# One PSUM bank a tile in the expert stage: first layers in two banks each, dense and expert halves of second layers in banks of their own

## The chip, the cores and the metric

The kernel is written in Bass with the Tile framework and runs on one core of a Trainium2 chip. The metric is the device time of one execution in microseconds (us). Before the change the median of three runs is 907.2 us (905.64 to 908.45).

The core's engines each work off their own queue of instructions in order: TensorE (PE) for matmuls, with its weight loads shown apart (PEld); VectorE (DVE); ScalarE (ACT); GpSimd (POOL); SyncE (SP), which here only starts transfers. They wait for each other through semaphores. TensorE writes its results into PSUM, which in this kernel is cut into eight banks of 128 partitions x 512 f32.

## The reference

Two stages, one after the other, over 8 batches of 2816 rows (22528 rows in all), with 256 channels and 64 query-key channels:

```python
# attention, for each batch
scores = (1 / S) * z @ z.T              # z: (2816, 64)
attn   = np.maximum(scores, 0.0) ** 2
x      = u * (attn @ v)                 # u, v: (2816, 256)

# mixture of experts over all rows x: (22528, 256)
y_dense    = np.maximum(x @ w1_dense, 0.0) @ w2_dense        # 256 -> 512 -> 256
logits     = x @ w_gate                                      # 8 experts
expert_idx = np.argmax(logits, axis=1)
gate_w     = softmax(logits)[row, expert_idx]
y_moe      = gate_w * (np.maximum(x @ w1[e], 0.0) @ w2[e])   # e = expert_idx of the row
out        = y_dense + y_moe
```

Each row thus goes through two networks of the same size, a dense one that all rows share, and one of eight experts.

## The kernel before

**Attention (up to about 560 us of the profiled execution).** Groups of rows are taken in turn. TensorE makes score blocks (L408), ScalarE and VectorE turn them into squared relus (L423 and L436, L425 and L438), TensorE multiplies them by `v` (L610), and VectorE multiplies the result by `u` into the row store `pays` (`gate_x`, L637). A planner written out by hand in the kernel (`offer`, `best`, `run`) gives each piece of elementwise work to the engine that it reckons to be free first. PSUM is used here as four pairs of banks (`banks`, tags `b0` to `b3`), which `take_pair` and `give_pair` hand round.

While the attention runs, rows whose expert is known are scattered into a table `xs` in DRAM that is sorted by expert (`scatter`, L761: an indirect DMA that GpSimd issues for each block of 128 rows). Two tables made on the device, `Rt` and `Et`, say for each tile of the next stage where its rows begin in `xs` and which expert it has.

**Expert stage (from about 560 us).** It is a sequence of slots, written out in Python in the order in which the engines work them off. The kernel fixes that order with `manual_schedule` for TensorE, ScalarE, VectorE and SyncE; GpSimd's order is left to the scheduler. There are two kinds of slot. The first 70 (`NT1`) take 256 rows of one expert, as two halves of 128 rows. Then come 21 units made of 128-row halves: 19 with two halves that may have different experts, 2 with one half. Two more units stand in an `If` that this data does not enter. That is 179 halves in all.

In slot s TensorE does four things in turn:

1. `up` with the dense weights: eight matmuls of 128x256 (L985) into a PSUM tile `h_ps`, then a relu on ScalarE (L988, 128x1024) into an SBUF ring;
2. `half(s - 2, 1)`, the second layer of the second half of the slot before last: four dense matmuls, then four expert matmuls (both L994);
3. `up` with the expert's weights, and its relu;
4. `half(s - 1, 0)`, the first half of the slot before.

After a `half`, its dense result is copied to SBUF (`yd`, L1011, ScalarE), then one VectorE instruction makes expert result x gate weight + dense result (L1012, `scalar_tensor_tensor`; this text calls it the combining instruction), and GpSimd sends the 128 rows to their places in the output (L1014, an indirect DMA). The order of the last two slots is a little different (`final`).

Beside this, VectorE copies the weights of the slot's expert from a store that holds all eight experts to a ring (`expert`, L972, 128x2048 bf16): one copy in a 256-row slot, two in a unit with two halves. In the 128-row units it also makes row indices (L1028). SyncE fetches the rows of a slot nine slots ahead, transposed (`fetch`, L936 to L950). GpSimd still has scatters of the last attention rows in every third slot, and short copies that hold it back (`pause`, L999). The SBUF rings hold 8 weight sets, 10 input tiles, 6 relu results, 3 dense results (`yd`) and 9 outputs (`ys`).

**PSUM in the expert stage.** Three of the pairs of banks stay from the attention as three tiles for first layers; `next_h` hands them round, so that a first layer takes the tile of the first layer three before. A tile of two banks holds a whole first layer (512 x 256 rows). The pair in which the last attention result lies is put last (`last_o`). The fourth pair is closed, and two tiles `yy` of one bank each take its place (`late["y"]`): the dense result of a half in the first 256 columns and the expert result in the other 256. A half takes the `yy` tile of the half before last. The last two groups of routing logits and counts borrow tiles of both kinds (`small`).

Of the kernel before, what the change touches and what calls it, by code (L numbers as in the profile page):

```python
# [15 lines left out]
P = 128  # L16
# [3 lines left out]
def kernel(  # L20
# [56 lines left out]
    mx = pool("mx", 6)  # L77
    NS = 4
    attention = ExitStack()
    ps = pool("ps", 1, space=bass.MemoryType.PSUM)  # L80
    top = attention.enter_context(tc.tile_pool(name="top", bufs=1, space=bass.MemoryType.PSUM))
    last_o = []
    late = {}

    def banks(x, name, shape=(P, 2, 4 * P), dt=F32):

        return (top if x == NS - 1 else ps).tile(list(shape), dt, name=name, tag=f"b{x}")


    wall = const.tile([P, E, WD], BF, name="wall")  # L90
# [492 lines left out]
    def av(n, i, between):  # L583
        b, i0, w = groups[n]
        if i == i0:
            turning.extend(far_steps(n))
        keep[0] = 0
        if n == 0 and i == i0:

            fill(n)  # L590
            need(n, 0)
        until(lambda: pairs[0][0] if pairs else None)
        ox = take_pair()
        o = banks(ox, "o")
        last_o[:] = [ox]
        for p in range(2):
            rest = list(range(nK))
            for x in range(nK):
                k = rest[0]
                if i == i0 and p == 0:  # L600

                    k = min(rest, key=lambda k: (max(key_at.get((n, k), 9e9), v_at(n, k)), k))
                    need(n, k)
                rest.remove(k)
                if n == 0 and i == i0 and p == 0 and x in (12, 14, 16):
                    load_u(2 * (x - 12) // 2, gate=True)
                for h in range(2):
                    r = slice(h * dq, (h + 1) * dq)
                    j = p ^ h
                    nc.tensor.matmul(out=o[:, j, 0:D], lhsT=block(n, k, i + j - i0)[r],  # L610
                                     rhs=v_of[b][r, k, :], start=(p == 0 and x == 0),
                                     stop=(p == 1 and x == nK - 1))
# [39 lines left out]
    def small(q, name, shape):  # L652
        if q < nQ - 2:
            return banks(bank_of[q], name, shape)
        if q == nQ - 1:
            return next_h(name, shape)
        return late["y"].tile(list(shape), F32, name=name, tag="y")

    def next_h(name, shape):
        late["h"].append(late["h"].pop(0))  # L660
        return banks(late["h"][-1], name, shape)

    def logits(q):
        n = sizes[q]
# [311 lines left out]
    def up(xT, ws):  # L976

        m = xT.shape[1]
        h_ps = next_h("h_ps", (P, 4, 2, P))
        n = m // len(ws)  # L980
        for i, w1 in enumerate(ws):
            hs = slice(i * n, (i + 1) * n)
            for f in range(4):
                for c in range(2):
                    nc.tensor.matmul(out=h_ps[:, f, hs, :], lhsT=w1(c, f), rhs=xT[:, hs, c, :],  # L985
                                     start=(c == 0), stop=(c == 1))
        h = take("h")
        nc.scalar.activation(h[:, :, 0:m * P], h_ps[:, :, 0:m, :].rearrange("p f h t -> p f (h t)"),  # L988
                             AF.Relu)
        return h  # L990

    def down(y, k, h, w2, j):
        for f in range(4):
            nc.tensor.matmul(out=y[:, k, :], lhsT=h[:, f, j * P:(j + 1) * P],  # L994
                             rhs=w2(f), start=(f == 0), stop=(f == 3))

    def pause(src):
# [5 lines left out]
    def half(s, j):  # L1003
# [1 line left out]
        hd, he, we, me, ids = pend[s]  # L1005
        we = we[j % len(we)]
        yd, ys = take("yd"), take("ys")
        y = late["y"].tile([P, 2, D], F32, name="yy", tag="y")
        down(y, 0, hd, lambda f: w2d[:, f, :], j)
        down(y, 1, he, lambda f: we[:, 2 * F + f * D:2 * F + (f + 1) * D], j)  # L1010
        nc.scalar.copy(yd, y[:, 0, :])  # L1011
        nc.vector.scalar_tensor_tensor(out=ys, in0=y[:, 1, :], scalar=me[:, j, 0:1],  # L1012
                                       in1=yd, op0=ALU.mult, op1=ALU.add)
        ins = nc.gpsimd.indirect_dma_start(  # L1014
            out=out, out_offset=bass.IndirectOffsetOnAxis(ap=ids[j], axis=0),
# [190 lines left out]
        jobs.pop(0)[1]()  # L1206
        run(9e9)
    attention.close()
    late["h"] = [x for _, x in pairs if x not in last_o + [NS - 1]] + [x for x in last_o if x < NS - 1]
    assert len(late["h"]) == NS - 1  # L1210
    late["y"] = pool("psY", 2, space=bass.MemoryType.PSUM)
    for s in range(NT - MAYBE + 2):
        assert s + AHEAD < NT1 or not waiting
        slot(s, NT - MAYBE)
# [45 lines left out]
```

## Time and profile before

| | |
|---|---|
| median of 3 runs | 907.2 us (905.64 to 908.45) |
| the profiled execution | 910.46 us |
| its span on the core | 908.8 us |
| mean granted clock of TensorE | 0.995 |
| instructions in the span | 30135 |
| busy: PE, PEld | 862.8 us (95%), 756.9 us (83%) |
| busy: DVE, ACT, POOL | 668.6 us (74%), 701.5 us (77%), 481.3 us (53%) |

The span goes from the first to the last instruction that the profiler saw on the core; the execution's own time holds what lies around it as well. Busy times leave out instructions that only wait, count or start transfers. The profile gives each group of instructions with its line, its engine, its tiles (out <- in) and what ended the idle time in front of it, which is called the releaser: `[1.15 <-DVE ring L1012]` behind an instruction means that its engine stood idle for 1.15 us before it, and that the wait ended when VectorE had finished the instruction of line 1012. `x4` in a row of the timeline means four instructions of one kind drawn together. Line numbers are those of the kernel before; the change moves the lines behind it up by a few.

### The profile page before, as it was taken

What the parts mean: (1) busy time and instruction counts of PE and PEld (TensorE: products, weight loads), DVE (VectorE), ACT (ScalarE), POOL (GpSimd) and SP (SyncE); (2) the same over time, 40 slices, a digit from 0 to 9 for tenths busy, and PEclk for the clock granted to TensorE, in tenths of its full rate; (3) what the DMA queues carried; (4) which work ended last, traced back from release to release, by engine and by line L of the source; (5) the groups of instructions that cost most, each with busy time, mean ns of one, the idle gap of its engine ahead of it and who ended that gap; (6) DMA issues with size and microseconds to landing.
All of it is one profiled execution on the core that took longest, in us unless ns stands there. A gap on an engine that the chain in (4) does not pass through costs nothing. (4 is left out here: it accounts for less than half of the span.)

```text
span 908.8 us, 30135 instructions
## 1 busy us (share of the span) xinstructions
PE 862.8 (95%) x12178; PEld 756.9 (83%) x12178; DVE 668.6 (74%) x1275; ACT 701.5 (77%) x873; POOL 481.3 (53%) x527
## 2 busy tenths in 40 slices
PE   7999999999999999999999979898989999999995
PEld 5898898798898898888888868787878878889894
DVE  8998798898888889889889974555544444446663
ACT  8998788788889889879879963666667667776764
POOL 7202353343353343353344434678788877777775
PEclk9999999999999999999999989999999999999999
DMA  8998999999999999999998858554545544444333
GB/s 173 175 195 153 201 178 175 201 172 184 209 179 183 203 172 185 206 187 172 199 169 171 153 105 125 114 119 107 108 111 107 116 108 114 112 104 97 96 92 88
DMA packets 289246, 136.80 MB, mean 151 GB/s; under 512 B 258638, under 2 KB 266062, under 8 KB 289104
## 3 DMA queue, kind: packets, MB, share of 16 engines
q1 hardware_dynamic: 263552, 79.40, 51.9%
q0 software_dynamic: 25552, 55.44, 26.1%
q8 instruction: 96, 1.57, 0.8%
q14 instruction: 46, 0.38, 0.1%
HBM read 61.54 MB, written 37.03 MB: 108 GB/s over the span
## 5 line engine op out<-in xcount | busy, mean ns | idle before, releaser
L610 PE MATMUL o<-vb,A 64*128 64x256 bf16 x7184 | 462.8, 270 | 3.2 <-DMA vb<-in_v_dram 1.5
L610 PEld LDWEIGHTS <-A 64*128 64x128 bf16 x7184 | 381.6, 94 | 46.8 <-issue 6.9
L761 POOL DMA_INDIRECT xs<-pays,pi x176 | 190.5, 1082 | 277.6 <-DVE pi L759 230.0
L423 ACT ACTIVATE r<-s 128x1024 f32<-128x1024 f32 (+1 forms) x246 | 242.4, 1009 | 52.4 <-PE s L408 49.3
L988 ACT ACTIVATE ring<-h_ps 128x1024 bf16<-128x1024 f32 x180 | 184.5, 1026 | 91.4 <-PE h_ps L985 47.7
L436 ACT ACTIVATE A<-r 128x1024 bf16<-128x1024 f32 (+1 forms) x246 | 248.6, 1041 | 3.8 <-issue 2.3
L1012 DVE SCALAR_TENSOR_TENSOR ring<-yy,me,ring 128x256 f32<-128x256 f32 x179 | 86.1, 482 | 146.9 <-ACT ring L1011 74.8
L425 DVE TENSOR_SCALAR r<-s 128x1024 f32<-128x1024 f32 x151 | 182.5, 1216 | 13.4 <-PE s L408 11.5
L1014 POOL DMA_INDIRECT out_dram<-ring,me x140 | 148.1, 1058 | 61.8 <-DVE ring L1012 30.4
L438 DVE TENSOR_TENSOR A<-r 128x1024 bf16<-128x1024 f32 x145 | 175.2, 1218 | 0.8
L994 PEld LDWEIGHTS <-ring 128*128 128x128 bf16 x1432 | 139.0, 98 | 38.4 <-issue 22.6
L408 PE MATMUL s<-zT 64*128 64x512 bf16 (+1 forms) x874 | 145.9, 356 | 8.9 <-remote 4.6
L994 PE MATMUL yy<-w2d,ring 128*128 128x256 bf16 x716 | 107.3, 272 | 17.6 <-DVE ring L1012 15.9
L994 PE MATMUL yy<-ring 128*128 128x256 bf16 x716 | 107.6, 273 | 0.2 <-issue 0.2
L985 PE MATMUL h_ps<-ring,w1d 128*128 128x256 bf16 x720 | 93.2, 272 | 2.7 <-DMA me<-xs 1.6
L985 PE MATMUL h_ps<-ring 128*128 128x256 bf16 (+1 forms) x872 | 93.8, 253 | 0.4 <-issue 0.2
L972 DVE COPY ring<-wall 128x2048 bf16 x109 | 83.1, 777 | 11.2 <-issue 7.5
L1011 ACT COPY ring<-yy 128x256 f32<-128x256 f32 x179 | 67.6, 378 | 28.1 <-PE h_ps L985 13.2
L637 DVE TENSOR_TENSOR pays<-o,ut 128x512 bf16<-128x512 f32 x88 | 60.3, 685 | 36.9 <-PE o L610 24.4
L985 PEld LDWEIGHTS <-ring 128*128 128x128 bf16 x872 | 73.5, 98 | 8.6 <-issue 0.9
L985 PEld LDWEIGHTS <-w1d 128*128 128x128 bf16 x720 | 69.6, 98 | 11.8 <-issue 3.9
L408 PEld LDWEIGHTS <-zT 64*128 64x128 bf16 x874 | 54.3, 94 | 23.4 <-issue 10.9
(123 smaller groups left out, 438.5 us busy)
## 6 DMA issues: line engine op xcount, KB each, us to landing
ut<-in_u_dram SPq DMA_DIRECT2D x88, 256.0 KB
vb<-in_v_dram POOLq DMA_DIRECT2D x14, 704.0 KB
wall<-in_moe_w_dram POOLq DMA_DIRECT2D x16, 256.0 KB
xs<-pays,pi POOLq DMA_INDIRECT x176
zr<-in_z_dram POOLq DMA_DIRECT2D x7, 352.0 KB
out_dram<-ring,me POOLq DMA_INDIRECT x140
ring<-xs SPq DMA_TRANSPOSE x114
xT<-pays SPq DMA_TRANSPOSE x88
```

The lines of the kernel that those rows point to most:

```text
L408: nc.tensor.matmul(out=s[:, h, y * c:(y + 1) * c], lhsT=zT[r, k + h, :], rhs=zT[r, i0:i0 + w, :], start=True, stop=True)
L423: nc.scalar.activation(r[:, :, :c], s[:, :, :c], AF.Relu, scale=1.0 / S)
L425: nc.vector.tensor_scalar(out=r[:, :, :c], in0=s[:, :, :c], scalar1=1.0 / S, scalar2=0.0, op0=ALU.mult, op1=ALU.max)
L436: nc.scalar.activation(a, r, AF.Square)
L438: (nc.gpsimd if eng == "pool" else nc.vector).tensor_mul(a, r, r)
L610: nc.tensor.matmul(out=o[:, j, 0:D], lhsT=block(n, k, i + j - i0)[r], rhs=v_of[b][r, k, :], start=(p == 0 and x == 0), stop=(p == 1 and x ...
L761: ins = nc.gpsimd.indirect_dma_start(out=xs, out_offset=bass.IndirectOffsetOnAxis(ap=pi[:], axis=0), in_=pays[:, g % (2 * G), 0:ROW].bitca ...
L985: nc.tensor.matmul(out=h_ps[:, f, hs, :], lhsT=w1(c, f), rhs=xT[:, hs, c, :], start=(c == 0), stop=(c == 1))
L988: nc.scalar.activation(h[:, :, 0:m * P], h_ps[:, :, 0:m, :].rearrange("p f h t -> p f (h t)"), AF.Relu)
L994: nc.tensor.matmul(out=y[:, k, :], lhsT=h[:, f, j * P:(j + 1) * P], rhs=w2(f), start=(f == 0), stop=(f == 3))
L1012: nc.vector.scalar_tensor_tensor(out=ys, in0=y[:, 1, :], scalar=me[:, j, 0:1], in1=yd, op0=ALU.mult, op1=ALU.add)
L1014: ins = nc.gpsimd.indirect_dma_start(out=out, out_offset=bass.IndirectOffsetOnAxis(ap=ids[j], axis=0), in_=ys, in_offset=None, bounds_chec ...
```

## The change

PSUM is given out in single banks in the expert stage. The attention's four pairs are closed altogether, and three pools of single banks take their place: four banks `h` for first layers, two banks `d` for dense results and two banks `e` for expert results.

- `up` takes two banks in turn, one for the first two blocks of 128 hidden channels and one for the last two. Each bank gets its own relu of 128x512 on ScalarE as soon as its matmuls are done. The matmuls stay as they were. Four banks are two layers' worth.
- `half` takes a bank for the dense result and one for the expert result. The dense result is copied to SBUF by VectorE (`tensor_copy`) and no longer by ScalarE, and that copy is written between the dense and the expert matmuls.
- `small` takes a bank `e` for the routing group before the last, and a bank `h` for the last one. `last_o` and `next_h` go.

Sizes, rings, weight copies, transfers and the slot order stay. The number of relus in the expert stage doubles, each of half the size; the number of matmuls, combining instructions and transfers does not change.

```diff
-    ps = pool("ps", 1, space=bass.MemoryType.PSUM)
-    top = attention.enter_context(tc.tile_pool(name="top", bufs=1, space=bass.MemoryType.PSUM))
-    last_o = []
+    ps = attention.enter_context(tc.tile_pool(name="ps", bufs=1, space=bass.MemoryType.PSUM))
...
     def small(q, name, shape):
         if q < nQ - 2:
             return banks(bank_of[q], name, shape)
-        if q == nQ - 1:
-            return next_h(name, shape)
-        return late["y"].tile(list(shape), F32, name=name, tag="y")
-
-    def next_h(name, shape):
-        late["h"].append(late["h"].pop(0))
-        return banks(late["h"][-1], name, shape)
+        return one_bank("h" if q == nQ - 1 else "e", name, shape[1:])
+
+    def one_bank(tag, name, shape):
+        t = late[tag].tile([P, 4 * P], F32, name=name, tag=tag)
+        return t[:, :shape[0] * shape[1]].rearrange("p (a b) -> p a b", b=shape[1])
...
     def up(xT, ws):
         m = xT.shape[1]
-        h_ps = next_h("h_ps", (P, 4, 2, P))
         n = m // len(ws)
-        for i, w1 in enumerate(ws):
-            hs = slice(i * n, (i + 1) * n)
-            for f in range(4):
-                for c in range(2):
-                    nc.tensor.matmul(out=h_ps[:, f, hs, :], lhsT=w1(c, f), rhs=xT[:, hs, c, :],
-                                     start=(c == 0), stop=(c == 1))
         h = take("h")
-        nc.scalar.activation(h[:, :, 0:m * P], h_ps[:, :, 0:m, :].rearrange("p f h t -> p f (h t)"),
-                             AF.Relu)
+        for f0 in (0, 2):
+            h_ps = one_bank("h", "h_ps", (2, 2 * P))
+            for i, w1 in enumerate(ws):
+                for f in (0, 1):
+                    for c in range(2):
+                        nc.tensor.matmul(
+                            out=h_ps[:, f, i * n * P:(i + 1) * n * P].rearrange("p (h t) -> p h t", t=P),
+                            lhsT=w1(c, f0 + f), rhs=xT[:, i * n:(i + 1) * n, c, :],
+                            start=(c == 0), stop=(c == 1))
+            nc.scalar.activation(h[:, f0:f0 + 2, 0:m * P], h_ps[:, :, 0:m * P], AF.Relu)
         return h
...
         yd, ys = take("yd"), take("ys")
-        y = late["y"].tile([P, 2, D], F32, name="yy", tag="y")
-        down(y, 0, hd, lambda f: w2d[:, f, :], j)
-        down(y, 1, he, lambda f: we[:, 2 * F + f * D:2 * F + (f + 1) * D], j)
-        nc.scalar.copy(yd, y[:, 0, :])
-        nc.vector.scalar_tensor_tensor(out=ys, in0=y[:, 1, :], scalar=me[:, j, 0:1],
+        dense, expert_ = (one_bank(x, "yy" + x, (1, D))[:, 0, :] for x in "de")
+        down(dense, hd, lambda f: w2d[:, f, :], j)
+        nc.vector.tensor_copy(yd, dense)
+        down(expert_, he, lambda f: we[:, 2 * F + f * D:2 * F + (f + 1) * D], j)
+        nc.vector.scalar_tensor_tensor(out=ys, in0=expert_, scalar=me[:, j, 0:1],
                                        in1=yd, op0=ALU.mult, op1=ALU.add)
...
     attention.close()
-    late["h"] = [x for _, x in pairs if x not in last_o + [NS - 1]] + [x for x in last_o if x < NS - 1]
-    assert len(late["h"]) == NS - 1
-    late["y"] = pool("psY", 2, space=bass.MemoryType.PSUM)
+    for x, n in (("h", 4), ("d", 2), ("e", 2)):
+        late[x] = pool("ps" + x, n, space=bass.MemoryType.PSUM)
```

In the 128-row units with two experts the first layer's order changes within the slot: channel blocks 0 and 1 with the first expert's weights, then with the second's, then blocks 2 and 3 with the first's, then with the second's. Before, all four blocks of the first expert came ahead of those of the second.

More of the change, by code (lines that the diff above doesn't have):

```diff
@@ L79 @@
     attention = ExitStack()
-    ps = pool("ps", 1, space=bass.MemoryType.PSUM)
-    top = attention.enter_context(tc.tile_pool(name="top", bufs=1, space=bass.MemoryType.PSUM))
-    last_o = []
+    ps = attention.enter_context(tc.tile_pool(name="ps", bufs=1, space=bass.MemoryType.PSUM))
     late = {}
     def banks(x, name, shape=(P, 2, 4 * P), dt=F32):
-        return (top if x == NS - 1 else ps).tile(list(shape), dt, name=name, tag=f"b{x}")
+        return ps.tile(list(shape), dt, name=name, tag=f"b{x}")
     wall = const.tile([P, E, WD], BF, name="wall")
@@ L594, in av @@
         o = banks(ox, "o")
-        last_o[:] = [ox]
         for p in range(2):
@@ L978, in up, with down @@
         m = xT.shape[1]
-        h_ps = next_h("h_ps", (P, 4, 2, P))
         n = m // len(ws)
-        for i, w1 in enumerate(ws):
-            hs = slice(i * n, (i + 1) * n)
-            for f in range(4):
-                for c in range(2):
-                    nc.tensor.matmul(out=h_ps[:, f, hs, :], lhsT=w1(c, f), rhs=xT[:, hs, c, :],
-                                     start=(c == 0), stop=(c == 1))
-        h = take("h")
-        nc.scalar.activation(h[:, :, 0:m * P], h_ps[:, :, 0:m, :].rearrange("p f h t -> p f (h t)"),
-                             AF.Relu)
+        h = take("h")
+        for f0 in (0, 2):
[8 more added lines that the diff above has]
+            nc.scalar.activation(h[:, f0:f0 + 2, 0:m * P], h_ps[:, :, 0:m * P], AF.Relu)
         return h
-    def down(y, k, h, w2, j):
+    def down(y, h, w2, j):
         for f in range(4):
-            nc.tensor.matmul(out=y[:, k, :], lhsT=h[:, f, j * P:(j + 1) * P],
+            nc.tensor.matmul(out=y, lhsT=h[:, f, j * P:(j + 1) * P],
                              rhs=w2(f), start=(f == 0), stop=(f == 3))
```

## The prediction

> **What bounds the kernel now.** I read the windows first, cut where the expert stage begins (560 us) and where its pace changes.
>
> ```profile
> span 908.8 us, 30135 instructions
> 560.00:760.00 200.00, 181.81 (x1646) 158.81 (x1643) 102.10 (x234) 131.55 (x204) 152.44 (x180) 1.00 0.50 111
> 760.00:820.00 60.00, 60.00 (x550) 53.60 (x549) 29.55 (x51) 43.40 (x69) 45.97 (x52) 1.00 0.44 108
> 820.00:880.00 60.00, 59.35 (x660) 54.24 (x658) 39.74 (x79) 41.95 (x69) 45.37 (x50) 1.00 0.39 95
> 880.00:909.00 29.00, 19.14 (x199) 15.44 (x197) 12.71 (x28) 12.70 (x23) 16.77 (x18) 0.95 0.34 89
> ```
>
> The columns are stretch, length, then busy time of PE, PEld, DVE, ACT and POOL, the granted clock, DMA share and GB/s. The diff leaves everything before 560 us as it is. Behind it TensorE is idle for 18.2 us up to 760, not at all up to 820, and for 0.65 us up to 880. So the change can win at most some 19 us and a little of the tail; everything else is matmul time, which it keeps: TensorE, POOL and SP get the same kinds of instructions in the same order.
>
> What TensorE waits for, from the table of waits over the run:
>
> ```profile
> PE yy L994 <- DVE ring L1012: 15.9, 18, 1.9
> PE h_ps L985 <- DMA me<-xs: 1.6, 1, 1.6
> ```
>
> So 15.9 us, in 18 waits, are the second layer waiting for a `yy` tile that VectorE has not read yet. Why that comes late is seen in the timeline, first where all is calm, then in a stretch with waits:
>
> ```profile
> 759.39 0.60 PE L994 MATMUL yy<-w2d,ring 128*128 128x256 bf16 x4
> 759.82 0.60 PE L994 MATMUL yy<-ring 128*128 128x256 bf16 x4
> 760.26 1.04 PE L985 MATMUL h_ps<-ring 128*128 128x256 bf16 x8
> 760.51 0.37 ACT L1011 COPY ring<-yy 128x256 f32<-128x256 f32 x1
> 760.96 0.48 DVE L1012 SCALAR_TENSOR_TENSOR ring<-yy,me,ring 128x256 f32<-128x256 f32 x1 [1.02 <-ACT ring L1011]
> 762.88 0.38 PE L994 MATMUL yy<-w2d,ring 128*128 128x256 bf16 x2
> ...
> 744.64 0.60 PE L994 MATMUL yy<-w2d,ring 128*128 128x256 bf16 x4
> 745.08 0.60 PE L994 MATMUL yy<-ring 128*128 128x256 bf16 x4
> 745.51 1.04 PE L985 MATMUL h_ps<-ring,w1d 128*128 128x256 bf16 x8
> 746.96 0.60 PE L994 MATMUL yy<-w2d,ring 128*128 128x256 bf16 x4 [0.41 <-DVE ring L1012]
> 747.40 0.60 PE L994 MATMUL yy<-ring 128*128 128x256 bf16 x4
> 748.41 0.37 ACT L1011 COPY ring<-yy 128x256 f32<-128x256 f32 x1
> 749.92 1.02 ACT L988 ACTIVATE ring<-h_ps 128x1024 bf16<-128x1024 f32 x1 [1.14 <-PE h_ps L985]
> 751.40 0.37 ACT L1011 COPY ring<-yy 128x256 f32<-128x256 f32 x1 [0.46 <-PE h_ps L985]
> 752.40 0.60 PE L994 MATMUL yy<-w2d,ring 128*128 128x256 bf16 x4 [1.15 <-DVE ring L1012]
> ```
>
> Calm: the half's last matmul ends at 760.42, ScalarE's copy starts 0.09 later, VectorE is done at 761.44, and the next half but one, which takes the same tile, starts at 762.88: a slack of 1.44 us. In the other stretch the copies at 748.41 and 751.40 belong to the halves that end at 745.68 and 748.00: 2.7 and 3.4 us later, with ScalarE idle before most of these instructions and waiting for TensorE. TensorE's signal is seen late. What delays it no row shows; but lateness above the slack turns into TensorE's wait.
>
> **The change, part by part.**
>
> *yy split, copy on VectorE.* Removed: ScalarE's copy, which could start only when the whole half was done. Added: a VectorE copy of 128x256 f32 out of PSUM. The trace has that only in small (a group, then one row of the timeline), and a heavier operation of the full size:
>
> ```profile
> L729 DVE COPY tb<-pre 128x88 f32<-128x88 f32 x14 | 3.3, 236 | 0.0
> 542.46 0.21 DVE L729 COPY tb<-pre 128x64 f32<-128x64 f32 x1
> L1012 DVE SCALAR_TENSOR_TENSOR ring<-yy,me,ring 128x256 f32<-128x256 f32 x179 | 86.1, 482 | 146.9 <-ACT ring L1011 74.8 <-issue 53.0 <-ACT ring L988 7.7
> ```
>
> 24 elements more cost 0.026 us, so 256 elements cost about 0.236 + 168 x 0.00108 = 0.42 us; the bounds are 0.24 and 0.48. [...]
>
> In the calm case the dense quarter ends at 759.99, the copy runs 760.08 to 760.50, the combining instruction 760.54 to 761.02. The expert bank is wanted at 762.88 + 0.44 = 763.32 (slack 2.3), the dense one at 762.88 (slack 2.4). Against 1.44 that is about 0.75 more after paying for the new copy, 18 x 0.75 = 13.5 us if every wait shrinks by that. The lower bound is 0, if lateness simply grows for as long as TensorE runs. I take 0.5 for each, near the 0.44 of dense matmuls that may now go ahead of a late expert bank: -9 us.
>
> *h in four single banks.* A first layer used to have three tiles in turn, now two tiles' worth: it waits for the relu of the layer before last, where the relu of the one before that had been waited for anyway by a second layer. A relu of half the size is in the trace:
>
> ```profile
> L988 ACT ACTIVATE ring<-h_ps 128x1024 bf16<-128x1024 f32 x178 | 183.3, 1031 | 91.2 <-PE h_ps L985 47.6 <-PE yy L994 30.6 <-issue 8.9
> 899.62 0.60 ACT L988 ACTIVATE ring<-h_ps 128x512 bf16<-128x512 f32 x1 [0.18 <-PE h_ps L985]
> L1011 ACT COPY ring<-yy 128x256 f32<-128x256 f32 x179 | 67.6, 378 | 28.1 <-PE h_ps L985 13.2 <-PE yy L994 13.0 <-DVE ring L972 0.8
> ```
>
> ScalarE's slot goes from 2 x 1.03 + 2 x 0.38 = 2.82 us to 4 x 0.60 = 2.40, of 3.49 that the matmuls take (four times 0.87, 744.64 to 745.51: eight matmuls for each of two layers and two halves): no bound. The layer at 760.26 would have its banks read by 761.5 and 762.1, and they are wanted at 763.75 and 764.19: slack 2.1 us. In calm this is hidden; with signals 2.7 to 3.4 us late it waits. Behind such a wait on TensorE's queue stands the whole next half. Bounds: 0, and 18 x 0.69 (relu and its start) = 12 us. Mostly TensorE would wait then for yy as well, so I take +1.5.
>
> *VectorE's load.* The rows of the 128-row slots (the first line is a group of 820 to 880), in which two weight copies stand between the two combining instructions:
>
> ```profile
> L985 PE MATMUL h_ps<-ring,w1d 128*128 128x256 bf16 x136 | 17.6, 273 | 0.0
> ...
> 843.54 0.48 DVE L1012 SCALAR_TENSOR_TENSOR ring<-yy,me,ring 128x256 f32<-128x256 f32 x1 [0.76 <-ACT ring L988]
> 844.26 1.33 DVE L972 COPY ring<-wall 128x2048 bf16 x2 [0.23 <-issue]
> 845.59 1.05 DVE L1012 SCALAR_TENSOR_TENSOR ring<-yy,me,ring 128x256 f32<-128x256 f32 x2
> 847.01 1.60 DVE L972 COPY ring<-wall 128x2048 bf16 x2 [0.37 <-issue]
> 848.61 0.47 DVE L1012 SCALAR_TENSOR_TENSOR ring<-yy,me,ring 128x256 f32<-128x256 f32 x1
> ```
>
> From the combining instruction in front of the weight copies to the one behind them: 845.59 - 843.54 = 2.05 and 848.61 - 846.16 = 2.45 us. With 0.40 for the second one (0.48 less the overlap of queued instructions, an estimate) and two copies at 0.46 each, a slot costs VectorE 3.37 to 3.77, middle 3.57, where TensorE's slot takes 3.53 (136 dense first-layer matmuls, 8 a slot, are 17 slots in 60 us). In 19 such slots: 0 to 19 x 0.24 = 4.6, I take +1.0. Before 820 a slot has one weight copy: 29.55 + 34 halves x 0.42 = 44 of 60, no bound (34 halves: 60 over the 1.745 of half a slot).
>
> *The start of the stage.* The first layer's bank now lies where the last attention output was:
>
> ```profile
> 560.14 1.05 PE L985 MATMUL h_ps<-ring,w1d 128*128 128x256 bf16 x8
> 561.05 0.69 DVE L637 TENSOR_TENSOR pays<-o,ut 128x512 bf16<-128x512 f32 x1 [1.69 <-PE o L610]
> 573.74 1.03 PE L985 MATMUL h_ps<-ring,w1d 128*128 128x256 bf16 x8 [1.58 <-DMA me<-xs]
> ```
>
> It waits for the multiplication that ends at 561.74, 1.6 us later than it starts now; the wait of 1.58 for a load at 573.74 takes that up. 0 to 1.6, I take 0.
>
> *The end.* The last halves' copies no longer stand in a row behind the expert matmuls: 0.4 us, ScalarE's copy, from the chain that ends the run; 0 to 0.9, I take -0.4.
>
> **Sum:** -9 + 1.5 + 1.0 + 0 - 0.4 = -6.9 us. The profiled execution took 910.46 us (span 908.8), 3.3 above the median of 907.2, whose runs reach from 905.64 to 908.45; the terms are differences, so they go onto the median: 900.3, forecast 900.
>
> **Rivals.** *The waiting moves.* If TensorE's signals are held back until it stops, it stops at `h_ps` instead of `yy`, and relu and copies then take as long as the old chain. For it: ScalarE is late too, with its 1.14 of waiting ahead of the relu at 749.92. Against: from 760 to 820 lateness went away with TensorE never idle. 907.
>
> *VectorE becomes the bound.* Place: the 128-row slots and the queue that now holds both releases of yy besides the weight copies. If a slot costs it the upper 3.77, those 4.6 us are lost there; and if its order keeps dense releases behind combining instructions that themselves wait, the 9 us don't come. 907.2 + 4.6 = 912. It decides once VectorE's slot is above TensorE's 3.53. For it: the middle, 3.57, is there already. Against: 70 of 91 slots have one weight copy for two halves of 3.49 us.
>
> *More signals, later signals.* TensorE now signals 8 times a slot (each bank of a layer, each half of a second layer) in place of 4. If what makes signals late is their number, the 15.9 us of waits double: 923. For it: the lateness is of TensorE's signals alone. Against: nothing shows that it counts signals.
>
> [...]
>
> **Numbers.** Forecast 0.46 (its own range 893 to 904), waiting moves 0.14, VectorE 0.22, later signals 0.12, cost per signal 0.06. A measurement of this kernel can tell some 0.3%, 2.7 us, from no change: faster 0.46, same 0.14, slower 0.40. The range 893 to 917 leaves out 923 and the far ends.
>
> **What would show it.** Right: waits of yy for VectorE fall from 15.9 to about 7 us, few and short waits of h_ps for ACT, relus of 0.60, copies near 0.42, TensorE idle under 12 us from 560 to 880. Wrong: h_ps waits for ACT above 5 us; idle time of TensorE in 820 to 880 above 3 us with VectorE over 55 of 60 busy; copies that start later than 3.4 us behind their matmuls.

## The result, and the profile after

The changed kernel is slower, by 0.7%: its median is 915.96 us over 17 runs (909.12 to 922.2), that of the kernel before 910.61 over 17 runs taken with them (905.34 to 919.57). The ratio is 1.0068, 95% interval 1.004 to 1.0096. The forecast was 900 in a range of 893 to 917, with 0.46 on faster: the time lies in the range, on the other side of no change.

The profiled execution took 915.24 us, 4.8 more than that of before. From the page of the changed kernel:

```profile
span 913.5 us, 30654 instructions
...
L985 ACT ACTIVATE ring<-h_ps 128x512 bf16<-128x512 f32 x360 | 193.9, 597 | 156.3 <-PE h_ps L981 86.9
...
L1008 DVE SCALAR_TENSOR_TENSOR ring<-yye,me,ring 128x256 f32<-128x256 f32 x179 | 86.6, 484 | 45.4 <-PE yyd L990 13.3
...
L1006 DVE COPY ring<-yyd 128x256 f32<-128x256 f32 x179 | 74.5, 416 | 43.2 <-PE h_ps L981 21.6
```

The single prices are as forecast: relus of 0.597, copies of 0.416. To see where the time went, both executions are cut at the same slots: 0 to 54 (in which GpSimd still has scatters), 54 to 70 (the other 256-row slots), 70 to 87 (128-row units), and the rest up to the last matmul. The columns are as in the prediction. First the kernel before, then the changed one:

```profile
560.10:769.00 208.90, 190.71 (x1727) 166.87 (x1726) 106.63 (x242) 138.13 (x214) 159.50 (x188) 1.00 0.49 111
769.00:825.10 56.10, 56.10 (x515) 50.10 (x513) 27.26 (x48) 40.22 (x65) 42.62 (x48) 1.00 0.44 108
825.10:886.20 61.10, 60.41 (x682) 55.12 (x680) 41.89 (x84) 41.45 (x67) 46.80 (x52) 1.00 0.39 96
886.20:901.00 14.80, 12.75 (x130) 9.99 (x128) 7.35 (x17) 9.05 (x16) 8.61 (x9) 1.00 0.38 94
```

```profile
560.80:771.30 210.50, 195.30 (x1725) 165.78 (x1725) 143.02 (x345) 116.06 (x217) 156.89 (x187) 1.00 0.46 109
771.30:828.60 57.30, 56.84 (x515) 50.01 (x513) 38.63 (x81) 34.77 (x65) 41.43 (x48) 1.00 0.45 107
828.60:893.40 64.80, 62.54 (x683) 55.03 (x681) 54.74 (x118) 37.30 (x68) 48.12 (x52) 1.00 0.37 91
893.40:906.60 13.20, 12.20 (x130) 10.28 (x127) 10.34 (x25) 5.91 (x13) 8.61 (x9) 1.00 0.43 100
```

The differences are +1.6, +1.2, +3.7 and -1.6 us; the stage starts 0.6 later, and from the last matmul to the end it is 0.8 shorter. Together 4.7, the difference of the spans (913.5 and 908.8). Slots 0 to 54, in which 9 us were to be won, won nothing. The largest loss is in the 128-row units, where VectorE is now busy for 54.74 of 64.80.

The waits of TensorE in the changed kernel show what became of the 15.9 us:

```profile
PE yye L990 <- DVE ring L1008: 7.4, 9, 1.2
PE h_ps L981 <- ACT ring L985: 4.7, 12, 1.1
PE h_ps L981 <- issue: 0.9, 3, 0.4
```

The wait for VectorE fell to 7.4 us, about as forecast (7). But first layers now wait as well. PE's busy time hides short stops, since a record of 0.27 us overlaps the next matmul, 0.109 behind it. So this text counts gaps: every distance from the start of one matmul of the stage to the start of the next that is above 0.15 us, less 0.109 (where the granted clock was at half, less 0.218). Before, slots 0 to 54 had 22.2 us of gaps, 19.3 of them ahead of second layers and 2.9 ahead of first layers. After, they had 23.9: 11.9 and 12.0. A gap counts to the stretch in which it begins.

### The profile page after: what moved, and what is told of

It reads as the page before. It is cut to its first block, busy times and chain, and to the rows that moved or that the text cites. A ratio compares the mean times of both kernels' runs of the same rounds, so it can differ in the third digit from the quotient of the medians.

```text
span 913.5 us, 30654 instructions
## 1 busy us (share of the span) xinstructions
PE 869.0 (95%) x12178; PEld 754.0 (83%) x12178; DVE 733.3 (80%) x1454; ACT 665.8 (73%) x874; POOL 480.1 (53%) x527
## 5 line engine op out<-in xcount | busy, mean ns | idle before, releaser
L985 ACT ACTIVATE ring<-h_ps 128x512 bf16<-128x512 f32 x360 | 193.9, 597 | 156.3 <-PE h_ps L981 86.9
L1010 POOL DMA_INDIRECT out_dram<-ring,me x140 | 144.5, 1032 | 68.9 <-DVE ring L1008 32.4
L990 PEld LDWEIGHTS <-ring 128*128 128x128 bf16 x1432 | 138.9, 98 | 29.9 <-issue 12.7
L1008 DVE SCALAR_TENSOR_TENSOR ring<-yye,me,ring 128x256 f32<-128x256 f32 x179 | 86.6, 484 | 45.4 <-PE yyd L990 13.3
L990 PE MATMUL yye<-ring 128*128 128x256 bf16 x716 | 107.5, 272 | 8.7 <-DVE ring L1008 7.4
L1006 DVE COPY ring<-yyd 128x256 f32<-128x256 f32 x179 | 74.5, 416 | 43.2 <-PE h_ps L981 21.6
L990 PE MATMUL yyd<-w2d,ring 128*128 128x256 bf16 x716 | 107.4, 272 | 0.6 <-DVE ix L1024 0.5
L981 PE MATMUL h_ps<-ring 128*128 128x256 bf16 (+1 forms) x872 | 97.0, 254 | 4.9 <-ACT ring L985 1.3
L981 PEld LDWEIGHTS <-ring 128*128 128x128 bf16 x872 | 72.6, 98 | 19.3 <-DVE ring L967 6.4
```

The lines of the kernel that those rows point to most:

```text
L981: nc.tensor.matmul(out=h_ps[:, f, i * n * P:(i + 1) * n * P].rearrange("p (h t) -> p h t", t=P), lhsT=w1(c, f0 + f), rhs=xT[:, i * n:(i + ...
L985: nc.scalar.activation(h[:, f0:f0 + 2, 0:m * P], h_ps[:, :, 0:m * P], AF.Relu)
L990: nc.tensor.matmul(out=y, lhsT=h[:, f, j * P:(j + 1) * P], rhs=w2(f), start=(f == 0), stop=(f == 3))
L1008: nc.vector.scalar_tensor_tensor(out=ys, in0=expert_, scalar=me[:, j, 0:1], in1=yd, op0=ALU.mult, op1=ALU.add)
L1010: ins = nc.gpsimd.indirect_dma_start(out=out, out_offset=bass.IndirectOffsetOnAxis(ap=ids[j], axis=0), in_=ys, in_offset=None, bounds_chec ...
```

## The experiments

Gaps of TensorE in us by slots, from one profiled execution of each kernel, and the ratio of its times to those of the kernel before on the same chip. Some executions had an attention some 12 us longer than others; only the expert stage of a profile is compared here.

| run | 0-54 | 54-70 | 70-87 | ratio (95%) |
|---|---|---|---|---|
| before | 22.2 | 0.2 | 1.1 | |
| changed | 23.9 | 1.4 | 4.1 | 1.0068 (1.004 to 1.0096) |
| e1 copy on ScalarE | 23.2 | 0.4 | 1.6 | 1.0029 (0.9987 to 1.0072) |
| e2 before, copy on VectorE | 22.0 | 0.1 | 2.0 | 1.0042 (1.0002 to 1.0082) |
| e3 only first layers changed | 20.1 | 1.3 | 1.3 | 1.0029 (0.9993 to 1.0066) |
| e4 second layers changed, two first-layer tiles | 23.6 | 0.0 | 3.2 | 1.0012 (0.9973 to 1.0051) |
| e5 before, no holding copies | 23.5 | 1.5 | 8.9 | 1.0054 (1.002 to 1.0087) |
| e6 changed, no holding copies | 23.5 | 2.2 | 2.9 | 1.0083 (1.0048 to 1.0118) |
| e7 before, two holding copies | 11.0 | 5.2 | 2.1 | one run, 919.42 us |
| e8 before, scatters in every slot | 19.5 | 0.0 | 0.4 | one run, 912.39 us |
| e9 before, two holding copies to slot 54 | 23.9 | 1.7 | 1.4 | 0.9989 (0.9949 to 1.003) |
| e10 changed, the same | 12.4 | 7.1 | 3.6 | 1.0001 (0.9963 to 1.0039) |
| e11 e1, the same | 12.3 | 6.9 | 2.4 | 0.999 (0.9954 to 1.0026) |
| e12 changed, old order of experts | 26.8 | 2.3 | 4.5 | one run, 926.55 us |
| e13 before, more transfers in 54-70 | 0.0 | 0.0 | 0.7 | one run, 878.88 us |
| e14 before, more copies in 54-70 | 0.0 | 0.0 | 7.5 | one run, 883.51 us |
| e15 changed, again | 0.4 | 0.0 | 2.9 | 1.0046 (1.0011 to 1.0081) |
| e16 changed, copy on ScalarE in 128-row units | 0.4 | 0.0 | 0.0 | 1.001 (0.9979 to 1.0042) |
| e17 before, again | 0.3 | 0.0 | 0.0 | 0.9976 (0.9939 to 1.0013) |
| e18 e16, again | 0.4 | 0.0 | 0.0 | 0.9994 (0.9956 to 1.0032) |

### The parts of the change: e1 to e4

The theory was that VectorE's load costs the time in the 128-row units, and that the waits up to slot 54 only move. The rivals were the depth of the first layers' banks, and the new order of the experts' matmuls in the units.

e1: in `half` of the changed kernel

```diff
-        nc.vector.tensor_copy(yd, dense)
+        nc.scalar.copy(yd, dense)
```

> The changed kernel with the dense copy back on ScalarE, everything else as changed. In the changed kernel's trace a 128-row slot takes 3.77 us where it took 3.51 to 3.53 before, VectorE goes from one instruction to the next without waiting there, and up to 760 us TensorE's gaps (start to start above 0.15 us, less one matmul) add up to 23.9 us against 22.2 before. If VectorE's load is what cost the time: 128-row slots back at 3.5 us, some 4 to 5 us faster than the changed kernel, so level with the kernel before within 2 us. If it is the order of the two experts' matmuls in those slots, which asks for the second weight copy four matmuls sooner: slots stay at 3.7 or more and the time stays within 1.5 us of the changed kernel. If the late signals alone decide the rest: gaps up to 760 us stay between 20 and 26 us.

e2: in the kernel before

```diff
-        nc.scalar.copy(yd, y[:, 0, :])
+        nc.vector.tensor_copy(yd, y[:, 0, :])
```

> The kernel before with the dense copy on VectorE behind the whole half, PSUM as before. If VectorE's load is what cost the time: 128-row slots at 3.7 to 3.8 us and 4 to 6 us slower than the kernel before, of which all lies behind 800 us. If the order of the experts' matmuls is: slots stay at 3.5 and the time within 1.5 us of the kernel before. Up to 760 us the copy no longer queues behind relus, so the waits for yy should shrink by 0 to 5 us if ScalarE's queue was part of them, and stay at 20 or more if TensorE's late signals alone are.

e3: the changed kernel with `half` as it was

```diff
-        dense, expert_ = (one_bank(x, "yy" + x, (1, D))[:, 0, :] for x in "de")
+        yy = one_bank("e", "yy", (2, D))
+        dense, expert_ = yy[:, 0, :], yy[:, 1, :]
         down(dense, hd, lambda f: w2d[:, f, :], j)
-        nc.vector.tensor_copy(yd, dense)
         down(expert_, he, lambda f: we[:, 2 * F + f * D:2 * F + (f + 1) * D], j)
+        nc.scalar.copy(yd, dense)
```

> Only the first layers changed: four single banks, a relu a bank; dense and expert result in one bank, copied by ScalarE behind the half as before. If two layers' worth of banks in place of three is a cost of its own: waits of first layers for relus of 5 us and more on top of the old waits for yy, 4 to 10 us slower than before. If the waiting only moves: waits for relus take the place of waits for yy, the gaps up to 760 us stay between 20 and 26, and the time is within 2 us of the kernel before. 128-row slots: 3.5 if VectorE's load sets them, 3.7 if the order of matmuls does.

e4: the changed kernel with first layers in two tiles of two banks, one relu each, and e1's copy

```diff
-        for f0 in (0, 2):
-            h_ps = one_bank("h", "h_ps", (2, 2 * P))
+        h_ps = one_bank("h", "h_ps", (4, 2 * P))        # tag h: 2 tiles of 2 banks
...
-            nc.scalar.activation(h[:, f0:f0 + 2, 0:m * P], h_ps[:, :, 0:m * P], AF.Relu)
+        nc.scalar.activation(h[:, :, 0:m * P], h_ps[:, :, 0:m * P], AF.Relu)
```

> Only the second layers changed: dense and expert banks of their own, two each; copy on ScalarE, written between dense and expert matmuls; first layers in two tiles of two banks with one relu of 128x1024 each and the old order of matmuls. My prediction's step gives -9 us for the split, less what two tiles in place of three cost. If the waiting only moves: waits of first layers for relus replace those for yy, gaps up to 760 us of 20 to 26, time within 2 us of the kernel before. If it is the split relus that bring waits through more signals: gaps up to 760 us well below 20 and 3 to 8 us faster than before.

Up to slot 54 the gaps stay between 20.1 and 23.6 us in all four, while what TensorE waits for changes with the layout. The largest waits of e2, e3 and e4, from the table of waits behind 545 us:

```profile
PE yy L994 <- DVE ring L1012: 15.0, 18, 2.0
```

```profile
PE yy L990 <- DVE ring L1009: 14.7, 18, 2.2
PE h_ps L981 <- ACT ring L985: 1.4, 4, 0.5
```

```profile
PE h_ps L981 <- ACT ring L985: 16.0, 14, 2.4
PE yye L990 <- DVE ring L1008: 0.8, 2, 0.5
```

e4 comes nearest to the forecast's step by itself, the split of `yy`; it also leaves first layers two tiles in place of three. It does nearly end the waits for VectorE: 15.9 us became 0.8. In their place 16.0 us of waits of first layers for relus came up, and the gaps went from 22.2 to 23.6. The waiting moves. That it stops at the PSUM tile that is shortest of room fits all four runs, but how much of the 16.0 us comes from the third tile that is missing no run shows. e3 shows that two layers' worth of banks for first layers is no cost next to the old `yy`: 1.4 us of waits for relus.

In the 128-row units, steady slots take 3.51 us in the kernels with the copy on ScalarE. e2 came out between its two expectations, with 3.55 and 3.73 in turn. The changed kernel's are at 3.72 to 3.81. Its timeline of VectorE shows a slot in which it never waits for another engine's late result for more than 0.2 us:

```profile
855.19 0.48 DVE L1008 SCALAR_TENSOR_TENSOR ring<-yye,me,ring 128x256 f32<-128x256 f32 x1 [0.20 <-PE yyd L990]
855.90 1.50 DVE L967 COPY ring<-wall 128x2048 bf16 x2 [0.23 <-issue]
857.32 0.15 DVE L1024 TENSOR_TENSOR ix<-me,inv 128x2 int32<-128x2 int32 x1
857.39 0.41 DVE L1006 COPY ring<-yyd 128x256 f32<-128x256 f32 x1
857.91 0.48 DVE L1008 SCALAR_TENSOR_TENSOR ring<-yye,me,ring 128x256 f32<-128x256 f32 x1
858.31 0.41 DVE L1006 COPY ring<-yyd 128x256 f32<-128x256 f32 x1
858.93 0.48 DVE L1008 SCALAR_TENSOR_TENSOR ring<-yye,me,ring 128x256 f32<-128x256 f32 x1 [0.20 <-PE yyd L990]
859.66 1.55 DVE L967 COPY ring<-wall 128x2048 bf16 x2 [0.25 <-issue]
```

From weight copy to weight copy are 3.76 us: the two weight copies, row indices, two copies and two combining instructions, 0.23 us ahead of the weight copies, and 0.20 between the second copy and the instruction that reads its result. The copies run 1 to 3 us behind their matmuls here, 2.1 in the median, and the gaps of TensorE sit ahead of expert first layers (4.1 of 4.1 us), which read the weights that VectorE copies.

The times of these four differ from before by less than or about as much as their intervals; the verdicts rest on the profiles. That e1 is 4 to 5 us faster than the changed kernel, as expected, its times cannot tell; slots 70 to 87 take 61.6 us in e1, where they took 64.8.

### What makes the signals late: e5 to e11

In the kernels so far TensorE's signals (the updates of its semaphore that the trace records) come late where GpSimd goes from one indirect transfer to the next, and in bursts when it waits: in the kernel before, between 575 and 750 us, 0.62 updates a us while a transfer is being issued, 0.99 during GpSimd's copies and 1.5 otherwise. Only TensorE's are late: in the same stretch a combining instruction starts at most 0.09 us behind the ScalarE copy that it waited for, and a TensorE that stopped goes on 0.05 behind the combining instruction, while ScalarE's copies start up to 4.7 us behind their matmuls, up to 2.0 of it with ScalarE idle (in e17, the same kernel on another chip, 0.09 in all). The theory was that GpSimd's load decides the gaps. e5 and e6 take the holding copies away, e7 doubles them, e8 moves the scatters to the front:

```diff
e5, e6  (kernel before, changed kernel)
-        if j == 0 and s < NT - MAYBE - 5:
-            pause(ys)
...
-            pause(pays[:, g % (2 * G), 0:ROW].bitcast(F32))
e7  (kernel before)
-        if j == 0 and s < NT - MAYBE - 5:
+        if s < NT - MAYBE - 5:
e8  (kernel before)
-        if s % 3 == 1 and waiting:
+        if s > 0 and waiting:
```

> The kernel before without GpSimd's two kinds of holding copies (0.4 to 0.9 us after each first half, 0.3 to 0.7 after each scatter). In the traces TensorE's semaphore updates fall behind where GpSimd goes from one instruction to the next without waiting, and come in a burst as soon as GpSimd waits. Theory GpSimd: those 22 us of TensorE's gaps up to slot 54 are what GpSimd's load costs. Without the copies GpSimd has per slot two outputs of some 1.3 to 1.5 us and a third of a scatter, 3.3 us of 3.49: gaps fall below 10 us, the time by 8 to 18 us. Rival, signals are late for another reason (TensorE's own): gaps stay at 20 to 26 and the time within 3 us of before. Rival, transfers: outputs are issued sooner and closer together, gaps grow.

> The changed kernel without the holding copies on GpSimd. Theory GpSimd: gaps up to slot 54 fall from 23.9 to below 10 us; what is left against the kernel before without them is VectorE's load in the 128-row slots, 3.7 to 3.8 us a slot, so 3 to 5 us. Rivals as for the kernel before: gaps stay at 20 to 26, or grow.

> The kernel before with a holding copy after both halves of each slot in place of the first alone: GpSimd gets 0.4 to 0.9 us more a slot. Theory GpSimd: TensorE's gaps up to slot 54 grow from 22 to 35 to 60 us, and between slots 54 and 70, where there were 0.2 us of gaps, 3 to 12 us appear. Rival, TensorE's own reason: gaps as before, 20 to 26 and below 2.

> The kernel before with the scatters of the last rows in every slot in place of every third, so that they are done by about slot 22 in place of 54. Theory GpSimd: gaps gather in the first 25 slots, 15 to 30 us in all, and slots 25 to 54 have below 3 us, where the kernel before has 10 to 12. Rival, TensorE's own reason: slots 25 to 54 keep 8 us and more.

The theory in this form fell. Less work for GpSimd left the gaps at 23.5 us; the kernel before even lost 8.9 us in the 128-row units. More work, e7, halved them up to slot 54, with 5.2 us coming back up to slot 70. e8 showed a link to the scatters: 19 of its 19.5 us lie in the first 25 slots, and slots 25 to 85 lost 0.8. That could still be used, so the second holding copy was tried up to slot 54 alone (`if (j == 0 or s < 54) and s < NT - MAYBE - 5`), in the kernel before, in the changed one, and in e1:

> The kernel before with the second holding copy on GpSimd only up to slot 54, as long as scatters go. With it in all slots TensorE's gaps up to slot 54 were 11.0 us in place of 22.2, and 6.5 us came up between slots 54 and 70. Theory: what holds TensorE's signals back is GpSimd issuing one indirect transfer right behind another, so a pause between all of them halves the loss: gaps 9 to 14 us up to slot 54 and below 2 us up to 70, the time 6 to 12 us below the kernel before. Rival, that run was a chance: gaps at 20 to 26 and the time within 3 us of before.

> The changed kernel with the same second holding copy up to slot 54. If GpSimd's issuing decides the gaps whatever the layout of PSUM: 9 to 14 us up to slot 54 in place of 23.9, and against the kernel before with that copy it stays 3 to 6 us slower, which is VectorE's load in the 128-row slots (3.7 to 3.8 us each). If split banks do help once signals are only a little late: gaps at 3 to 8 us.

> The changed kernel with the second holding copy up to slot 54 and the dense copy on ScalarE. If the two causes are GpSimd's issuing and VectorE's load, both are gone: gaps of 9 to 14 us up to slot 54, 128-row slots at 3.5 to 3.6, the time level with the kernel before with that copy within 3 us and 6 to 12 us below the kernel before without it. If split relus and banks cost by themselves: 3 us and more above the kernel before with that copy.

Nothing was gained on the kernel before: ratios of 0.9989, 1.0001 and 0.999, each with 1 in its interval. e9's gaps are the old ones, so e7's 11.0 was no effect that comes back in every execution. Where gaps were small (e7, e10, e11), GpSimd's outputs up to slot 54 ran 7.5 to 11.5 us behind the combining instructions in the median and 12 to 16 at most, where the median is 0.3 to 2.8 in the other runs so far, and 5 to 7 us of gaps followed between slots 54 and 70. Against the rival of e10, split banks brought no gaps of 3 to 8 us either. e10's own expectation, 3 to 6 us more than e9, does not show in the times (the ratios are 0.1% apart, each known to 0.4%), though its units take 3.72 to 3.82 us.

e12 is the changed kernel with `for f in range(4)` inside the loop over experts, and both relus behind it:

> The changed kernel with the old order of the two experts' first layers in the 128-row slots: all four blocks of the first, then of the second, into the same two banks, both relus behind that. VectorE's work is as in the changed kernel. If VectorE's load alone sets the 3.77 us of a slot: 3.70 to 3.80. If half of it is the second weight copy that is asked for four matmuls sooner: 3.60 to 3.68, as where the old kernel had its copy on VectorE (3.55 and 3.73 in turn).

The steady units took 3.73 to 3.82 us: the order is not what makes them slow. That VectorE's work is, the next runs show.

### Without late signals: e13 to e18

> The kernel before with one more indirect transfer of 128 rows of 576 bytes in each slot from 54 to 69, to a tensor of its own that nobody reads (the size of a scatter, about 1.3 us of GpSimd with its start). In every run so far the slots up to 54, in which 17 scatters go, lose 17 to 27 us together with those up to 70, and the slots after the last scatter lose almost nothing. If a scatter costs TensorE some 1.3 us as an indirect transfer: 16 of them bring 12 to 25 us of gaps between slots 54 and 70, where there were 0.2. If only GpSimd's time counts: the same here and with copies of the same length. If neither: below 3 us.

> The kernel before with three more copies on GpSimd in each slot from 54 to 69, about 1.3 us a slot as in the run with one more transfer, but no transfer. If GpSimd's time is what TensorE pays: 12 to 25 us of gaps between slots 54 and 70, perhaps later, when the outputs' ring of nine is full. If the transfer itself, or its issuing, holds TensorE's signals back: below 4 us up to slot 70 beyond what a full ring brings, and TensorE's signals on time.

> The changed kernel once more, on the same chip as the next one. Gaps of 20 to 27 us up to slot 54, 128-row slots in the steady part at 3.72 to 3.81; some 0.7% slower than before.

> The changed kernel with the dense copy on ScalarE in the 128-row slots alone, on VectorE in the 70 others. If VectorE's load in those 19 slots is what the change costs: slots there at 3.5 to 3.6, 3 to 5 us faster than the changed kernel, and within 3 us of the kernel before. If the change costs in the slots up to 54: as slow as the changed kernel.

The edits: e13 issues one more indirect transfer after a first half, `if j == 0 and 54 <= s < 70`, from `ys[:, 0:ROW // 2]` to a tensor of its own; e14 three more `pause(ys)` in its place; e15 is the changed kernel as it is; e16 has

```diff
-        nc.vector.tensor_copy(yd, dense)
+        (nc.vector.tensor_copy if s < NT1 else nc.scalar.copy)(yd, dense)
```

These four ran on another chip than the first twelve, which were spread over three, and there the kernel before takes 872.3 us (23 runs, 868.75 to 880.09). So it was itself profiled on one more chip, beside e16 again:

> The kernel before itself once more. On the last chip TensorE's signals came on time and the slots up to 54 lost nothing (186.5 us in place of 208.9), in a kernel that is the one before up to there. If late signals belong to the chip or to the run and not to the kernel: this run has either gaps of 20 us and more up to slot 54 and a time above 900 us, or below 2 us and a time near 872, and the next one, on the same chip, has the same.

> The changed kernel with the copy on ScalarE in the 128-row slots, once more. With late signals: gaps of 20 us and more up to slot 54, as in the kernel before beside it, 128-row slots mostly at 3.51, time within 4 us of before. Without: below 2 us, and within 2 us of before.

The kernel before took 870.41 us in its ten runs there, 873.25 in 23 others beside them, and has no late signals. e15's expected gaps of 20 us and more did not come either. The windows of e17, e15 and e16, cut at slots 0, 54, 70, 87 and the end:

```profile
561.00:748.00 187.00, 186.75 (x1727) 167.35 (x1726) 106.96 (x242) 137.66 (x214) 152.88 (x188) 1.00 0.60 124
748.00:803.80 55.80, 55.80 (x514) 50.02 (x512) 26.17 (x49) 41.09 (x65) 42.95 (x50) 1.00 0.46 111
803.80:863.60 59.80, 59.80 (x683) 55.16 (x682) 39.51 (x85) 43.83 (x69) 45.56 (x50) 1.00 0.39 96
863.60:875.00 11.40, 11.40 (x130) 10.39 (x127) 7.32 (x17) 8.05 (x15) 9.10 (x10) 1.00 0.53 119
```

```profile
560.40:747.30 186.90, 186.80 (x1724) 167.00 (x1724) 145.43 (x346) 116.83 (x218) 151.78 (x183) 1.00 0.56 123
747.30:803.20 55.90, 55.90 (x514) 50.10 (x513) 38.94 (x80) 34.73 (x65) 45.10 (x54) 1.00 0.46 116
803.20:866.70 63.50, 62.11 (x683) 55.08 (x682) 54.14 (x118) 36.95 (x69) 45.83 (x50) 1.00 0.37 92
866.70:879.00 12.30, 11.70 (x129) 10.29 (x127) 10.60 (x26) 5.66 (x13) 8.58 (x9) 1.00 0.41 106
```

```profile
547.90:734.90 187.00, 186.88 (x1725) 167.06 (x1725) 146.15 (x346) 116.91 (x218) 151.84 (x184) 1.00 0.56 123
734.90:790.80 55.90, 55.90 (x515) 50.10 (x513) 39.00 (x80) 34.74 (x65) 45.36 (x53) 1.00 0.47 116
790.80:850.50 59.70, 59.70 (x683) 55.08 (x681) 43.40 (x89) 44.92 (x100) 47.20 (x51) 1.00 0.39 97
850.50:862.00 11.50, 11.50 (x130) 10.40 (x127) 7.25 (x17) 8.39 (x21) 9.19 (x9) 1.00 0.41 117
```

TensorE hardly stops in the kernel before, with 0.3 us of gaps: there was nothing to win. From the first to the last matmul the stage takes 313.9 us before, 318.7 in the changed kernel and 313.9 in e16 and e18. The change costs 3.7 us in slots 70 to 87 and 1.1 behind them, 4.8 in all; the medians of e15 and of before are 4.7 apart. Taking VectorE's copy out of the 128-row units, and nothing else, takes all of it back: e16 is at 872.53 us, beside 872.3 for the kernel before.

The timeline of e17, its rows of TensorE and ScalarE alone, shows a half with its signals on time:

```profile
744.02 0.60 PE L994 MATMUL yy<-ring 128*128 128x256 bf16 x4
744.46 1.04 PE L985 MATMUL h_ps<-ring,w1d 128*128 128x256 bf16 x8
744.71 0.37 ACT L1011 COPY ring<-yy 128x256 f32<-128x256 f32 x1
745.33 0.60 PE L994 MATMUL yy<-w2d,ring 128*128 128x256 bf16 x4
745.53 1.02 ACT L988 ACTIVATE ring<-h_ps 128x1024 bf16<-128x1024 f32 x1 [0.46 <-PE h_ps L985]
```

The half ends at 744.62 and is copied 0.09 us later; the first layer ends at 745.50 and its relu starts 0.03 later. From 575 to 750 us, 1.07 updates a us pass while GpSimd issues a transfer, and 1.2 while it does neither that nor a copy. These rates count what the trace recorded: 198 updates of TensorE in this stretch, 148 in the kernel before, so part of the difference is records that are missing. e13 and e14 cannot part their theories: signals were on time on this chip, and neither 16 more transfers nor 48 more copies bring gaps between slots 54 and 70. e13's run ends 12.7 us behind its last matmul, where e17's ends 7.2 behind. e14's 7.5 us come behind slot 70, when GpSimd was up to 19 us behind and VectorE waited for the outputs' ring, 6.0 us for GpSimd's copies and 5.0 for transfers.

What makes signals late is not settled. Shown is that the same kernel has 22.2 us of gaps in one execution and 0.3 in another on another chip, that all fourteen profiled executions of the first chips have late signals and none of the six of the two later ones, and that on the first chips the gaps come while scatters are issued. Whether the chip, the placement of data or something else decides, no run tells.

## Why the prediction was wrong

**What bounds the kernel.** The rows were read rightly: 18.2 us of idle TensorE, 15.9 of them waits for `yy`. The step that failed is what followed: that a wait at one tile can be won by giving that tile more slack. The rows that argued so, lateness of 2.7 to 3.4 us against a slack of 1.44, showed a cause outside the tile, and the text said that nothing shows what delays the signal. A cause that isn't known can't be priced at half its effect. What the runs showed in its place: waits for `yy` did fall, 15.9 to 7.4 us, but the gaps up to slot 54 stayed, 22.2 and 23.9 us, since first layers waited instead.

Of the signs named, the sign of being right that failed is TensorE's idle time from 560 to 880 us: 18.1 us, where under 12 was asked for. Of the signs of being wrong one came, 10 of 104 dense copies up to slot 54 more than 3.4 us behind their matmuls (4.9 at most); waits of `h_ps` for relus stayed just below their limit, 4.7 us of 5, and TensorE's idle time from 820 to 880 was 1.6 us, where 3 would have told.

**yy split, -9.** Wrong in kind on the first chips, and without object on the later ones. The 0.75 us for each wait, from which it took 0.5, does not come out of its own slacks either: 2.3 and 2.4 less 1.44 are 0.9. Gaps ahead of second layers fell by 7.4 us (19.3 to 11.9), close to the forecast, but those ahead of first layers rose by 9.1 (2.9 to 12.0). The rival "the waiting moves" describes this. Its counter-argument, that from 760 to 820 lateness went away with TensorE never idle, did not bear on the slots with scatters.

**h in four banks, +1.5 (0 to 12).** By itself it costs nothing that shows (e3: 20.1 us of gaps). Together with the split it took up the waiting, 9.1 us, within its bounds.

**VectorE, +1.0 (0 to 4.6).** The mechanism was right, the value was too low. A unit took 3.76 us, the upper end, in place of the middle of 3.57: 3.7 us in these units on the first chips, 3.7 and another 1.1 behind slot 87 on the later ones. The rival "VectorE becomes the bound" had this at 4.6 and a chance of 0.22. In the timeline the stretch from a combining instruction over the weight copies is near the middle of its bounds (857.39 - 855.19 = 2.20, of 2.05 to 2.45), and the mis-sized term is the two copies: 0.52 and 0.62 up to the start of the next instruction in place of 0.46 each. In e2, where both read one bank behind the whole half, the same copies took 0.45 and 0.50. So the price was right for a copy in a queue and too low in this layout; what the 0.20 us of idle time behind the second copy wait for stays open, as the profile names TensorE's dense matmuls in most units and the copy itself in others. The middle lay above TensorE's 3.53 already, so every tenth on top of it counted.

**The start, 0 (0 to 1.6), and the end, -0.4.** The stage started 0.9 us later behind the last attention matmul (0.20 before, 1.08 after). The tail was 1.6 shorter up to the last matmul and 0.8 behind it; on the later chips the same stretches are 1.1 longer and 0.8 shorter. So neither term is firm.

**More signals.** Neither form came in. Twice the signals did not double the waits (22.2 and 23.9 us of gaps). A cost per signal in matmul time, to which 0.06 of the chances and the upper end of the range, 917, belong, is shown by no run: in slots 0 to 54 without late signals the kernel before takes 187.0 us (e17) and the changed one 186.9 (e15), with 4 more signals in each slot, and in the rows at 744.64, 745.08 and 745.51 of the kernel before groups of four matmuls start 0.44 us apart without a signal between them and 0.43 with one.

With 0 in place of -9 + 1.5, 3.7 in place of 1.0 and the other terms as forecast, the sum would have been +3.3, 910.5, and slower the likeliest.

## What to carry to other kernels

A wait in the table names the tile at which an engine stops, not why its partner is late: before pricing more buffers, ask whether the partner was slow to work or slow to be told, and count stops ahead of every tile, since waiting can move, as it did in e4 (15.9 us ahead of `yy` became 0.8, and 16.0 came up ahead of `h_ps`). Work that is moved to an engine must be summed over its fullest stretch, not over the stage: 0.42 us twice in a slot was free in 70 slots and cost all of the difference in 21, where signals were on time. When runs of one kernel differ by as much as the effect, profile the old kernel more than once before explaining its idle time.

## What the runs showed of the hardware

The kernel before took 901 to 925 us on the first chips and 868 to 884 on the later two, with a mean granted clock of 0.98 to 1.00 in the profiles of both. Its expert stage took 340.8 us in one profile and 313.9 in the other, 27 us apart, 22 of them up to slot 54, where TensorE's signals come late. The rest of the distance between the medians of the two groups of chips lies by the profiles mostly ahead of the stage, which began at 548 to 572 us in the profiles of all runs. In e10 the granted clock was at half for 6.8 us within the expert stage (the second row), behind gaps of TensorE that add up to 4.0 us between 789 and 795; in e7 it was 0.97 in the mean from 769 to 832 us. The windows of e10:

```profile
780.00:794.90 14.90, 11.56 (x103) 9.73 (x100) 6.93 (x13) 5.61 (x10) 12.38 (x15) 1.00 0.39 111
794.90:801.70 6.80, 5.99 (x30) 4.03 (x28) 4.38 (x9) 3.53 (x7) 4.46 (x6) 0.50 0.42 109
801.70:808.00 6.30, 6.30 (x60) 5.63 (x59) 3.70 (x9) 4.18 (x8) 4.32 (x5) 1.00 0.32 89
```

At half, matmuls of e10 start 0.21 us apart in place of 0.109 (30 records in the 6.80 us of the second row, 60 in the 6.30 of the third), which cost 2.8 us more here. Whether the stop brought it on, these runs don't show.
